# Attention with landmarks and a feed-forward layer on one core: the DMA transposes of k and q issued as one piece, and a new order of all work

## The chip, the cores and the metric

The kernel runs on one core of a Trainium2 chip. The metric is the device time in microseconds (us), the median of several runs. The engines are TensorE (PE), VectorE (DVE), ScalarE (ACT), GpSimd (POOL) and SyncE (SP); POOL and SP here mostly issue DMA transfers.

## The reference

```python
def _attn_ref(q, k, v):                      # q, k, v: (8, 8, 576, 64) float32
    m = 32; scale = 1.0 / np.sqrt(D)
    q_lm = q.reshape(B, H, m, S // m, D).mean(axis=3)
    k_lm = k.reshape(B, H, m, S // m, D).mean(axis=3)
    # sm(a, b): softmax over the last axis of scale * a @ b^T
    A, Bm, C = sm(q, k_lm), sm(q_lm, k_lm), sm(q_lm, k)
    Z = Bm.transpose(0, 1, 3, 2) / (norm1(Bm) * norminf(Bm) + 1e-06)
    for _ in range(6):
        Z = 2 * Z - Z @ Bm @ Z
    return A @ Z @ C @ v
...
def _moe_ref(x, w_in, w_out):                # x: (4608, 512), w_in: (512, 2048), w_out: (2048, 512)
    h = x @ w_in
    return (h * (1.0 / (1.0 + np.exp(-h)))) @ w_out
```

`x` is the attention's output with the heads of a position laid side by side. So for each of 8 batches there are three softmaxes through 32 landmarks, six steps of a Newton iteration on 32 by 32 matrices, and two dense layers with a SiLU between.

## The kernel before, in words

**One program, one written order.** Every piece of work is an `Op` with a name: a kind, some digits for its part, and after the point its batch (`xt1.4`, `ltr0.3`), or after the at sign the place of a second-layer block (`p4@5120.0`). The function `attn` makes the pieces of a batch's attention, `layer1` those of the first dense layer (`h`, `g`), `layer2_pair` and `layer2_plain` those of the second (`ss`, `p`, `c`, `os`). The constant `SEQUENCE` lists the names in the order in which they are written into the program; a suffix such as `/ACT` says which engine does a piece that could run on two. `Plan.run` walks through this list and checks only that each piece stands behind what it depends on. The list was written out by a search over a model of the engines' times; the search itself isn't in the file. Since every engine runs its instructions in program order, the list fixes the order on PE, DVE, ACT, POOL's queue and SP's queue. A word `*n` stands for `n` dummy matmuls on zeros (84 in all, in the first part).

**The pieces that the transposes touch.** Batches 0 to 2 transpose k and q on PE (`tr`, `trc`). Batches 3 to 7 use DMA transposes, SP's line 533, which turn the loaded tile `qk` into `qT`: `xt1.b` for k, then `xt0.b` for q. Each is an operation of its own on SP with a planned time of 1.8 us and a lag of 3 us. It waits for the loads of its batch (`ld1.b`, `ld0.b`: k and q on POOL, line 396), for `ldv0.b` (the first of three loads of v, line 403; a rule written as "one kind of transfer at a time"), and for the pieces `A` and `C` two batches earlier, which read the same buffer. What follows a transpose:

- on DVE `lra`, `lrb`, `lrc`, `lrd` (line 571), the sums over positions that give the landmarks, into `red` and then `rs`; digit 1 for k, 0 for q;
- on PE `ltr` (a fold of `rs`), then `sb` and the chain of softmax, norm and Newton steps (`pb`, `bmx`, `ns`, `nsd`, `fb`);
- on PE `A` and `C`, which read `qT` itself, with `Ax`, `S`, `Ln`, `Rs`, `Cx` on ACT and PE and `etn` on DVE behind them;
- on SP `ct0.b` (line 813), a second DMA transpose, of the exponentials `ce`, from batch 2 on; PE's `cv0.b` multiplies its result with v.

SP's queue holds, in the list's order, these transposes and nearly all stores of the output (line 982). The loads of batch b+1 wait for the first transpose of batch b and, from batch 4's loads on, for the `ct0` of the batch before that one; the first load of v in batch b+2 also waits until `cv0.b` has read the buffer.

`mc` copies `m` out of PSUM on ACT or DVE; `u2`, `c1`, `c5`, `c21` copy second-layer products out, `c11`, `c12`, `c22` add to them on DVE. ACT loads another function table where it goes between exponentials (`Ax`, `Cx`, `Ln`, `Rs`, `pb`) and SiLU (`g`, `gx`).

Of the kernel before, what the change touches and what calls it, by code (L numbers as in the profile page):

```python
# [19 lines left out]
const ldk ld11.0 ident ld00.0 ld01.0 ld0.1 k0cDVE k0cACT ld1.1 fold k0 *18 lms100.0 lms106.0  # L20
ldv2.0 lms1012.0 *6 lms110.0 tr10.0 lms116.0 tr19.0 tr114.0 trc114.0/DVE *2 lms000.0 lms006.0
trc10.0/DVE lms0012.0 tr00.0 trc19.0/DVE lms1112.0 tr05.0 trc00.0/ACT trc05.0/DVE *2 tr09.0
lmc1.0/ACT lms010.0 lms016.0 trc09.0/DVE lms0112.0 ltr1.0 tr014.0 lmc0.0/ACT lmT1.0/DVE
trc014.0/ACT *3 ltr0.0 tr15.0 lmT0.0/DVE ld1.2 trc15.0/DVE *4 sb.0 C0.0 A0.0 ld0.2 tr00.1 Cx00.0
tr014.1 Ax00.0 lms000.1 ldv1.0 lms006.1 pb.0 Ax01.0 lms0012.1 pbs.0 A1.0 wi1b1 pbr.0 lms010.1
bmx.0 Ax11.0 lms016.1 bmt.0 wi0b0 csb.0 lms0112.1 Cx01.0 S01.0 bbd.0 n1.0 lmc0.1/ACT *2 f0.0
ldv0.0 nrm.0 trc00.1/ACT stz.0 *3 tr10.1 stf1.0 stf0.0 wi0b1 Ax10.0 fb00.0 fb01.0 trc10.1/ACT *3
ns00.0 trc014.1/DVE S00.0 S10.0 tr19.1 nsd00.0 Ln01.0 wi3b0 ns01.0 tr114.1 fb10.0 Ln10.0 ns10.0
Ln00.0 nsd10.0 nsd01.0 fb20.0 Rs0.0 fb11.0 *8 ns11.0 ns20.0 S11.0 ctm00.0 nsd11.0 trc114.1/ACT
nsd20.0 ltr0.1 fb21.0 fb30.0 Ln11.0 *1 ns21.0 ctc00.0/DVE lms100.1 tr15.1 Rs1.0 lms106.1 etn0.0  # L30
lms1012.1 lms110.1 wi1b0 lms116.1 trc19.1/ACT nsd21.0 lms1112.1 tr15.2 fb31.0 lmc1.1/DVE
lmT0.1/ACT ns31.0 trc15.2/ACT nsd31.0 *2 ltr1.1 trc15.1/DVE tr09.1 ns30.0 lmT1.1/DVE tr05.1 C1.0
fb41.0 nsd30.0 sb.1 trc05.1/ACT tr114.2 fb40.0 trc09.1/DVE pb.1 ns40.0 ns41.0 Cx11.0 pbs.1 *2
tr19.2 wi1a Cx10.0 pbr.1 nsd41.0 nsd40.0 bmx.1 trc19.2/ACT bmt.1 *4 csb.1 wi0a A1.1 etn1.0 A0.1
trc114.2/ACT tr00.2 wi2a Ax01.1 n1.1 ctm10.0 trc00.2/DVE Ax11.1 tr014.2 wi3b1 Ax00.1 nrm.1 bbd.1
ctc10.0/ACT stz.1 *3 f0.1 fb50.0 S00.1 wrc.0 C1.1 wi2b0 trc014.2/DVE Ln00.1 *1 cv0.0 fb51.0 Cx10.1
cv1.0 stf0.1 wi2b1 ns51.0 fb00.1 Ax10.1 tr10.2 wc.0 Cx11.1 ns00.1 ns50.0 S10.1 wi3a nsd51.0 S11.1
nsd00.1 S01.1 nsd50.0 Ln10.1 zbd.0 Ln01.1 wo0 fb10.1 trc10.2/DVE *5 ns10.1 Rs0.1 ctm10.1 nsd10.1
zt.0 tr09.2 lra1.2 ztc.0/ACT C0.1 wo1 Ln11.1 ctc10.1/DVE *1 m1.0 Cx00.1 mc11.0/DVE mc10.0/ACT *4
m0.0 tr05.2 ldv1.1 Cx01.1 mc00.0/DVE h4.0 mc01.0/ACT etn0.1 g4.0 *3 h3.0 ldv0.1 trc09.2/DVE h2.0  # L40
lrb1.2 ldv2.1 h0.0 lrc1.2 h5.0 trc05.2/DVE wo2 g0.0 ctm00.1 fb20.1 lrd1.2 g5.0 ns20.1 h7.0 wo3
nsd20.1 g3.0 ltr1.2 h1.0 fb30.1 ctc00.1/DVE lmT1.2/ACT ns30.1 h6.0 g1.0 ldv0.2 nsd30.1 m2.0 lra0.2
g2.0 m3.0 mc20.0/DVE mc21.0/ACT mc31.0/ACT lrb0.2 *7 h10.0 g6.0 lrc0.2 h8.0 lrd0.2 g7.0 fb40.1
h11.0 ldv1.2 mc30.0/DVE Rs1.1 ltr0.2 o0@5000.0 lmT0.2/DVE sb.2 h15.0 ns40.1 o0@5001.0 pb.2 nsd40.1
g11.0 ldv2.2 pbs.2 o1@5001.0 fb50.1 pbr.2 bmx.2 ld1.3 bmt.2 csb.2 ns50.1 o1@5000.0 bbd.2 n1.2
nrm.2 g10.0 nsd50.1 ld0.3 stz.2 f0.2 h12.0 g8.0 stf0.2 h9.0 fb00.2 g15.0 zbd.1 ns00.2 hx8.0 g9.0
nsd00.2 cv0.1 fb10.2 gx8.0 wrc.1 ns10.2 h13.0 ldv0.3 wc.1 g12.0 nsd10.2 zt.1 h14.0 fb20.2
ztc.1/ACT etn1.1 ns20.2 o2@5001.0 g14.0 ldv1.3 nsd20.2 g13.0 m3.1 m0.1 m1.1 o2@5000.0 mc00.1/ACT
mc01.1/DVE mc31.1/ACT mc30.1/DVE h2.1 mc10.1/ACT mc11.1/DVE ldv2.3 m2.1 o3@5000.0 mc21.1/ACT
mc20.1/DVE g2.1 ss00@5020.0 h7.1 h4.1 fb30.2 oc@5000.0/DVE h6.1 g4.1 wt00 ns30.2 h9.1 os@5000.0  # L50
h5.1 wt10 h12.1 g5.1 ss10@5020.0 h11.1 g12.1 o3@5001.0 ss20@5020.0 g11.1 g9.1 wt01 h14.1 h15.1
g6.1 nsd30.2 h13.1 fb40.2 g15.1 wt20 h0.1 g7.1 h3.1 wt30 g0.1 h10.1 oc@5001.0/DVE g13.1 h8.1
p1@5020.0 g3.1 wt11 os@5001.0 g10.1 wt21 h1.1 c1@5020.0/ACT xt1.3 p2@5020.0 g1.1 g8.1 p5@5020.0
c11@5020.0 g14.1 ss30@5020.0 xt0.3 C0.2 C1.2 c5@5020.0/DVE A0.2 Cx01.2 p6@5020.0 wt31 ss00@5100.0
p3@5020.0 ss10@5100.0 Ax00.2 p1@5120.0 Cx10.2 ss20@5100.0 Ax01.2 Cx11.2 S00.2 p1@5100.0
ss30@5100.0 Cx00.2 Ln00.2 lra1.3 ct0.2 hx8.1 u2@5020.0/ACT c12@5020.0 p7@5020.0 gx8.1 lrb1.3
lrc1.3 ns40.2 os@5020.0 hx0.0 c1@5100.0/DVE ss00@5120.0 p5@5100.0 l1done.0 nsd40.2 gx0.0
ss10@5120.0 S01.2 p6@5100.0 c1@5120.0/ACT fb50.2 c5@5100.0/ACT c22@5020.0 ld1.4 p2@5100.0 lrd1.3
u2@5100.0/ACT lra0.3 Ln01.2 ld0.4 p7@5100.0 lrb0.3 lrc0.3 p3@5100.0 c11@5100.0 lrd0.3 ltr0.3
ns50.2 ltr1.3 c12@5100.0 p2@5120.0 lmT0.3/ACT c22@5100.0 lmT1.3/ACT ss20@5120.0 sb.3 p4@5020.0  # L60
pb.3 nsd50.2 c11@5120.0 pbs.3 A1.2 C1.3 pbr.3 cv0.2 bmx.3 Ax10.2 ss30@5120.0 Cx11.3 p6@5120.0
ldv0.4 Rs0.2 bmt.3 bbd.3 zbd.2 ldv1.4 Cx10.3 p4@5100.0 wrc.2 Ax11.2 wc.2 ldv2.4 c21@5020.0/ACT
etn0.2 f0.3 u2@5120.0/ACT S11.2 os@5021.0 S10.2 csb.3 zt.2 Ln11.2 p5@5120.0 n1.3 os@5100.0
ztc.2/ACT nrm.3 c21@5100.0/DVE Ln10.2 stz.3 m1.2 Rs1.2 stf0.3 m2.2 fb00.3 C0.3 p7@5120.0
c5@5120.0/ACT mc21.2/DVE xt1.4 mc11.2/ACT etn1.2 Cx00.3 p3@5120.0 mc20.2/ACT c22@5120.0 Cx01.3
mc10.2/DVE ns00.3 h9.2 ct0.3 nsd00.3 h8.2 c12@5120.0 g9.2 m3.2 fb10.3 m0.2 p4@5120.0 mc01.2/DVE
os@5101.0 xt0.4 h7.2 mc31.2/ACT c21@5120.0/DVE ns10.3 h5.2 mc00.2/DVE g7.2 h6.2 g8.2 nsd10.3 h2.2
fb20.3 mc30.2/ACT h1.2 g2.2 h0.2 g5.2 ns20.3 ld1.5 h10.2 nsd20.3 g1.2 h14.2 fb30.3 ld0.5 h4.2 g0.2
ns30.3 h12.2 g14.2 nsd30.3 h3.2 g6.2 fb40.3 h15.2 g10.2 ns40.3 h13.2 g3.2 nsd40.3 h11.2 fb50.3
g4.2 lra1.4 hx8.2 g15.2 p1@5220.0 wrc.3 g12.2 lrb1.4 g13.2 lrc1.4 hx0.1 g11.2 ns50.3 p1@5200.0  # L70
l1done.1 nsd50.3 gx0.1 lrd1.4 ss00@5220.0 c1@5220.0/ACT A0.3 gx8.2 A1.3 zbd.3 p2@5200.0
ss10@5220.0 c1@5200.0/ACT Ax10.3 ss20@5220.0 p2@5220.0 c11@5200.0 lra0.4 p6@5220.0 Ax01.3 Ax11.3
lrb0.4 S10.3 cv0.3 lrc0.4 Ln10.3 S01.3 lrd0.4 Ax00.3 ss00@5200.0 ltr1.4 ldv0.5 ltr0.4 p5@5220.0
lmT1.4/ACT ldv1.5 ss30@5220.0 lmT0.4/ACT u2@5220.0/ACT sb.4 ldv2.5 wc.3 S00.3 p7@5220.0 pb.4
ss10@5200.0 c5@5220.0/ACT pbs.4 Ln00.3 S11.3 c11@5220.0 zt.3 p3@5220.0 Ln11.3 pbr.4 c22@5220.0
bmx.4 Rs1.3 ss20@5200.0 csb.4 p4@5220.0 ztc.3/ACT n1.4 Ln01.3 bmt.4 nrm.4 c12@5220.0 p5@5200.0
Rs0.3 bbd.4 os@5220.0 stz.4 ss30@5200.0 c21@5220.0/ACT xt1.5 f0.4 m3.3 c5@5200.0/ACT stf0.4 m1.3
C0.4 mc30.3/DVE p6@5200.0 mc10.3/ACT etn0.3 mc31.3/ACT p3@5200.0 os@5121.0 Cx01.4 fb00.4
mc11.3/DVE u2@5200.0/ACT os@5120.0 Cx00.4 m2.3 xt0.5 etn1.3 C1.4 m0.3 mc21.3/ACT p7@5200.0
mc20.3/DVE Cx11.4 c12@5200.0 mc01.3/ACT ns00.4 h14.3 os@5200.0 Cx10.4 nsd00.4 h4.3 mc00.3/DVE  # L80
g14.3 ct0.4 h11.3 fb10.4 h7.3 ns10.4 hx0.3 nsd10.4 h2.3 os@5221.0 fb20.4 g7.3 ns20.4 h0.3 gx0.3
nsd20.4 h8.3 fb30.4 g11.3 h1.3 g0.3 ns30.4 h10.3 nsd30.4 g2.3 h15.3 fb40.4 lra1.5 g8.3 hx0.2 ld1.6
g15.3 h3.3 lrb1.5 l1done.2 ld0.6 gx0.2 h5.3 lrc1.5 h9.3 wrc.4 g4.3 lrd1.5 p1@5340.0 g10.3 lra0.5
g3.3 h12.3 lrb0.5 g9.3 ltr1.5 h6.3 lrc0.5 g1.3 lrd0.5 h13.3 lmT1.5/DVE g5.3 hx8.3 c22@5200.0 g12.3
ns40.4 ltr0.5 p4@5200.0 l1done.3 g6.3 nsd40.4 lmT0.5/DVE g13.3 c1@5340.0/DVE sb.5 p1@5300.0 fb50.4
gx8.3 ss00@5300.0 pb.5 p2@5340.0 ss10@5300.0 ss20@5300.0 p5@5300.0 c11@5340.0 c21@5200.0/ACT
c1@5300.0/ACT A1.4 pbs.5 A0.4 pbr.5 cv0.4 Ax11.4 bmx.5 ss30@5300.0 Ax01.4 csb.5 p6@5300.0
c5@5300.0/ACT ldv0.6 bmt.5 Ax00.4 n1.5 bbd.5 ldv1.6 nrm.5 f0.5 stz.5 p3@5300.0 u2@5300.0/ACT
stf0.5 ldv2.6 Ax10.4 fb00.5 ss00@5320.0 ns00.5 p7@5300.0 nsd00.5 ss00@5340.0 S00.4 S11.4 p2@5300.0
wc.4 Ln00.4 fb10.5 ss10@5340.0 S10.4 p5@5340.0 xt1.6 c22@5300.0 Ln10.4 Ln11.4 ss20@5340.0 ns10.5  # L90
p4@5300.0 nsd10.5 fb20.5 c12@5300.0 S01.4 os@5201.0 ns50.4 p6@5340.0 Ln01.4 nsd50.4 c11@5300.0
# [1082 lines left out]
```

## Time and profile before

| | |
|---|---|
| median of 3 runs | 248.0 us (247.12 to 248.7) |
| the profiled execution | 249.88 us, its span 248.2 us |
| PE busy | 236.4 us (95%) |
| ACT, DVE, POOL busy | 185.9, 180.2, 36.9 us |
| mean granted clock of PE | 0.993 |
| DMA transposes `qT<-qk` on SP | 10, issue 2.55 to 4.37 us, median 5.2 us to landing (4.6 to 8.3) |
| DMA transposes `ct<-ce` on SP | 6, issue 1.41 to 2.08 us, median 3.8 us to landing |
| loads of v | 24, median 9.9 us to landing (6.3 to 14.2) |

In the profile's timelines a row gives the start, the length, the engine, the line, the operation and the tiles written and read; in brackets stands the idle time before it, and what ended it. "SPq" and "POOLq" rows are issues of transfers: the length is the time that the queue was held, not the transfer's. In the list of waits a row reads: who, line, for whom; total us, how often, longest.

### The profile page before, as it was taken

To read this page: it belongs to the slowest core of one execution; us is meant where nothing else is said; L and a number is where in the kernel's file an instruction comes from. 1 tells how busy PE (TensorE), PEld (TensorE's weight loads), DVE (VectorE), ACT (ScalarE), POOL (GpSimd) and SP (SyncE) were. 2 spreads that over 40 slices of the span, in tenths; PEclk is the share of its full clock that TensorE was granted. 3 is DMA by queue.
4 is the path that set the end of the run, shared out by engine and by line. 5 is a ranking of instruction groups with operands and counts; after the bars stand their busy time and mean duration, and the time that the engine had idled before them with its cause. 6 is when DMAs were issued, how large, how long until landed. Compare 5 with 4: busy or idle time off the path is not lost.

```text
span 248.2 us, 7298 instructions
## 1 busy us (share of the span) xinstructions
PE 236.4 (95%) x2968; PEld 167.7 (68%) x2968; DVE 180.2 (73%) x498; ACT 185.9 (75%) x439; POOL 36.9 (15%) x62
## 2 busy tenths in 40 slices
...
PEclk9999999999999999799999999999999999999999
...
GB/s 162 201 184 203 170 179 204 206 210 221 173 156 176 214 212 169 187 138 214 126 189 169 178 257 167 168 191 4 63 108 140 123 42 3 0 3 85 129 105 108
DMA packets 54210, 36.82 MB, mean 148 GB/s; under 512 B 34464, under 2 KB 46240, under 8 KB 54176
## 3 DMA queue, kind: packets, MB, share of 16 engines
...
## 4 chain that ended last, share of the span: by engine, by line
PE 66%; DMA 21%; ACT 7%; DVE 2%; issue 2%; POOL 1%; SPq 0%; POOLq 0%; DVEq 0%
PE ps L323 65%; DMA qT<-qk 6%; DMA v<-in_v_dram 5%; DMA qk<-in_q_dram 5%; ACT gm L912 3%; DMA w_in_sb<-in_moe_w_in_dram 3%; DMA qk<-in_k_dram 2%; DVE red L571 1%; ACT L912 1%; PE ps L511 1%; ACT pb L637 1%; ACT gx L937 1%; POOL w_in_sb L410 1%; ACT m L333 1%; ACT L1127 1%
## 5 line engine op out<-in xcount | busy, mean ns | idle before, releaser
L912 ACT ACTIVATE gm<-ps 128x512 f16<-128x512 f32 x128 | 67.9, 644 | 8.3 <-PE ps L323 7.9
L323 PE MATMUL ps<-etn,m 128*128 128x64 bf16 (+1 forms) x512 | 70.4, 286 | 0.2 <-DVE m L335 0.2
L323 PEld LDWEIGHTS <-gm 128*128 128x128 f16 x512 | 48.2, 98 | 12.1 <-issue 2.8
L323 PE MATMUL ps<-w_out_sb,gm 128*128 128x256 f16 (+1 forms) x392 | 54.4, 284 | 0.0
L323 PEld LDWEIGHTS <-m 128*128 128x128 bf16 x512 | 31.7, 98 | 22.7 <-issue 1.6
L323 PEld LDWEIGHTS <-ss 128*128 128x128 f16 x408 | 39.1, 99 | 6.1 <-issue 0.5
L333 ACT COPY ost<-ps 128x256 f32<-128x256 f32 x52 | 19.1, 385 | 21.0 <-PE ps L323 16.6
L323 PE MATMUL ps<-wt,ss 128*128 128x256 f16 x272 | 34.6, 273 | 0.0
L1044 DVE TENSOR_TENSOR ost<-ost,ps 128x256 f32<-128x256 f32 x51 | 20.7, 415 | 16.0 <-PE ps L323 8.3
L335 DVE CAST m<-ps 128x512 bf16<-128x512 f32 x35 | 23.4, 686 | 2.9 <-PE ps L323 2.6
L706 DVE SCALAR_TENSOR_TENSOR st<-st,ps 128x128 bf16<-128x128 bf16 (+2 forms) x54 | 13.6, 259 | 11.7 <-PE ps L323 9.4
L323 PE MATMUL ps<-w_out_sb,ss 128*128 128x256 f16 x136 | 18.3, 279 | 0.0
L333 ACT CAST m<-ps 128x512 bf16<-128x512 f32 x29 | 16.5, 608 | 1.7 <-PE ps L323 1.5
L748 ACT ACTIVATE ln<-ps 128x288 f32<-128x288 f32 x32 | 12.8, 421 | 6.7 <-PE ps L323 6.4
L396 POOL DMA_DIRECT2D qk<-in_k_dram x7 | 5.1, 724 | 83.7 <-DMA ct<-ce 53.8
L403 POOL DMA_DIRECT2D v<-in_v_dram x24 | 14.0, 587 | 23.2 <-PE ps L323 15.0
L1009 DVE TENSOR_TENSOR ss<-gm 128x1024 f16<-128x1024 f16 x15 | 10.3, 685 | 8.4 <-ACT gm L912 8.4
L323 PE MATMUL ps<-zer 128*128 128x256 bf16 x84 | 14.6, 306 | 1.1 <-DVE zer L430 1.1
L323 PE MATMUL ps<-wt,gm 128*128 128x256 f16 x120 | 15.6, 273 | 0.0
L681 DVE TENSOR_TENSOR fb<-st,hmask 128x256 bf16<-128x256 bf16 (+1 forms) x54 | 14.5, 274 | 1.1
L783 ACT ACTIVATE ce<-ps 128x288 bf16<-128x288 f32 x32 | 13.4, 423 | 2.1 <-PE ps L323 2.0
L738 ACT ACTIVATE et<-ps 128x288 bf16<-128x288 f32 x32 | 12.3, 420 | 2.0 <-PE ps L323 1.9
...
## 6 DMA issues: line engine op xcount, KB each, us to landing
...
qk<-in_q_dram POOLq DMA_DIRECT2D x7, 576.0 KB, 10.6
...
w_out_sb<-in_moe_w_out_dram POOLq DMA_DIRECT2D x4, 512.0 KB, 12.0
...
```

The source lines that it names most:

```text
L323: nc.tensor.matmul(out=out_ap, lhsT=lhsT, rhs=rhs, start=start, stop=stop, skip_group_check=True)
L333: nc.scalar.copy(out=out, in_=in_)
L335: nc.vector.tensor_copy(out=out, in_=in_)
L403: lambda e, a=a: nc.gpsimd.dma_start(out=v_r[b % 2][a * L:(a + 1) * L, :, :], in_=v[b].rearrange("h (l a x) d -> a l h (x d)", l=L, a=VA)[ ...
L681: nc.vector.tensor_tensor(out=fb[it % 2][:, g0:g1], in0=bc(sr[it % 3][:, g0:g1, 0:L], 4, 2), in1=bc(hmask, n, 1), op=OP.mult), [o], 14.5 + ...
L706: nc.vector.scalar_tensor_tensor(out=s2[:, g0:g1, lo:SW], in0=s[:, g0:g1, lo:SW], scalar=2.0, in1=ps[:, 0:NG * SW].rearrange("p (g x) -> p ...
L738: lambda e, g=g, et=et, c=c: nc.scalar.activation(out=et[:, c], in_=bank(me["A", g], c)[:, 0:HS], func=AF.Exp, scale=sc / J),
L748: lambda e, g=g, c=c, ln=ln: nc.scalar.activation(out=ln[:, c], in_=bank(me["S", g, c])[:, 0:HS], func=AF.Ln),
L783: nc.scalar.activation(out=ce[:, :, 0:VP].rearrange("p (i c) (a l) -> p c a i l", c=2, a=VA)[:, c], in_=bank(me["C", g], c)[:, 0:HS].rearr ...
L912: lambda e, dc=dc, cell=cell: nc.scalar.activation(out=gm[:, dc, :].rearrange("p (c l j) -> p c l j", c=2, l=L), in_=bank(cell["o"]).rearr ...
L1009: lambda e, o_=o_[:, k], x=x[:, k], y=y[:, k], op=op: nc.vector.tensor_tensor(out=o_, in0=x, in1=y, op=op), dep, 850.0 + prio / 100)
L1044: nc.vector.tensor_tensor(out=out_, in0=x, in1=y, op=OP.add)
```

## The change

The two DMA transposes of a batch become one operation `xt.b` with a planned time of 5.4 us, which issues k's and then q's, with nothing between them on SP. Those who read k's transpose wait, in the plan, for its end without a lag, those who read q's with the lag of 3 us. The loads of the next batch are planned against its end less 0.6 us; in the program they wait, as before, for the transpose of k. The whole list `SEQUENCE` is a new one: new places on every engine, 83 dummy matmuls, other engines for some copies (37 `mc` on ACT and 27 on DVE instead of 29 and 35; 7 `u2` on ACT and 10 on DVE instead of 13 and 4), 11 switches of ACT's table instead of 13, and another order of the first loads.

```diff
...
     def load(name, prio, us, issue, emit, deps=(), after=()):
-        d = list(deps) + list(after)
+        d = list(deps) + [(x, -0.6) if x.name[:2] == "xt" else x for x in after]
...
-            for t in (1, 0):
-                o = A(f"xt{t}.{b}", [("SP", 1.8)],
-                      lambda e, t=t: nc.sync.dma_start_transpose(
-                          out=qT[:, t].rearrange("p g j x -> p (g j) x"),
-                          in_=qk[:, t].rearrange("p g j d -> p (g j d)")),
-                      [qk_ops[b, t, g] for g in range(NG)] + use + gate, p0 + 5, lag=XLAG)
-                o.after = gate
-                qt_ops[t, 0] = qt_ops[t, 1] = [o]
-                me["qk_read"].append(o)
-                me["xts"].append(o)
+            o = A(f"xt.{b}", [("SP", 5.4)], lambda e: [nc.sync.dma_start_transpose(
+                out=qT[:, t].rearrange("p g j x -> p (g j) x"),
+                in_=qk[:, t].rearrange("p g j d -> p (g j d)")) for t in (1, 0)][0],
+                [qk_ops[b, t, g] for t in (1, 0) for g in range(NG)] + use + gate, p0 + 5, lag=XLAG)
+            o.after = gate
+            qt_ops[1, 0] = qt_ops[1, 1] = [(o, 0.0)]
+            qt_ops[0, 0] = qt_ops[0, 1] = [o]
+            me["qk_read"] = me["xts"] = [o]
...
-        gate = last[b - 1].get("xts", [])[:1]
+        gate = last[b - 1].get("xts", [])
...
```

Of the two lists, the stretches around batch 3's and batch 4's transposes and the end. Before:

```
... h1.1 c1@5020.0/ACT xt1.3 p2@5020.0 g1.1 g8.1 p5@5020.0
c11@5020.0 g14.1 ss30@5020.0 xt0.3 C0.2 C1.2 c5@5020.0/DVE A0.2 Cx01.2 ...
... c5@5120.0/ACT mc21.2/DVE xt1.4 mc11.2/ACT etn1.2 Cx00.3 p3@5120.0 mc20.2/ACT c22@5120.0 Cx01.3
mc10.2/DVE ns00.3 h9.2 ct0.3 nsd00.3 h8.2 c12@5120.0 g9.2 m3.2 fb10.3 m0.2 p4@5120.0 mc01.2/DVE
os@5101.0 xt0.4 h7.2 ...
... p3@5740.0 c21@5740.0/ACT os01@5741.0/ACT os00@5741.0/SP c12@5740.0 os10@5740.0/ACT os11@5740.0/SP
```

After:

```
... g15.1 h1.1 xt.3 c1@5020.0/ACT p2@5020.0 g1.1 g9.1 p6@5020.0 ...
stz.3 g9.2 u2@5120.0/DVE f0.3 h5.2 stf0.3 g15.2 xt.4 h8.2 fb00.3 ns00.3 ... hx8.1 fb30.3 ...
fb40.3 h3.2 ct0.3 ns40.3 ...
... p4@5700.0 c11@5700.0 os0@5700.0/SP c21@5700.0/ACT os0@5701.0/SP
```

More of the change, by code (lines that the diff above doesn't have):

```diff
@@ L19 @@
 SEQUENCE = """
[L20 to L91, printed above, removed]
@@ L98 @@
-Cx01.5 lrb0.6 ztc.4/ACT ct0.5 lrc0.6 p3@5320.0 c21@5340.0/ACT lrd0.6 c21@5320.0/ACT c11@5320.0
-Rs1.5 wrc.5 ltr0.6 m3.4 c12@5320.0 lmT0.6/ACT m0.4 os@5321.0 m1.4 mc30.4/DVE mc31.4/ACT ns50.5
-os@5341.0 sb.6 mc00.4/ACT mc10.4/DVE h12.4 pb.6 h14.4 mc11.4/DVE os@5320.0 g12.4 h15.4 pbs.6
-nsd50.5 ld1.7 h13.4 mc01.4/DVE h6.4 pbr.6 ld0.7 h3.4 bmx.6 bmt.6 g14.4 m2.4 bbd.6 cv0.5 zbd.5 g6.4
-mc21.4/DVE h0.4 g13.4 ldv0.7 wc.5 csb.6 g15.4 h1.4 n1.6 ldv1.7 mc20.4/DVE f0.6 g0.4 zt.5 h5.4
-ldv2.7 g1.4 ztc.5/DVE h7.4 nrm.6 g3.4 m1.5 stz.6 m3.5 stf0.6 g7.4 h4.4 fb00.6 mc10.5/DVE g5.4
@@ L146 @@
-os01@5741.0/ACT os00@5741.0/SP c12@5740.0 os10@5740.0/ACT os11@5740.0/SP
+const ldk ld11.0 ident ld00.0 ld01.0 ld0.1 k0cACT k0cDVE ld1.1 k0 *18 tr15.0 lms100.0 tr10.0
+trc15.0/DVE lms106.0 lms1012.0 trc10.0/ACT *9 lms110.0 lms116.0 lms1112.0 tr19.0 lmc1.0/DVE
+tr114.0 trc114.0/DVE *4 tr05.0 fold tr00.0 lms000.0 ltr1.0 lms006.0 lms0012.0 lmT1.0/DVE
+trc05.0/DVE *3 lms010.0 lms016.0 lms0112.0 tr014.0 tr09.0 lmc0.0/DVE trc014.0/ACT *1 ltr0.0 ld1.2
+trc00.0/ACT lmT0.0/DVE trc09.0/DVE ld0.2 *6 C0.0 A0.0 trc19.0/DVE sb.0 Cx00.0 ldv0.0 *2 C1.0 pb.0
@@ new lines @@
+lms000.1 Ax01.0 pbs.0 tr09.1 Cx11.0 ldv1.0 pbr.0 lms006.1 bmx.0 S01.0 csb.0 bmt.0 ldv2.0 Ln01.0
+bbd.0 n1.0 Cx10.0 *5 f0.0 wi2a tr00.1 nrm.0 Cx01.0 stz.0 ctm10.0 stf0.0 trc09.1/ACT wi0b1
+lms0012.1 fb00.0 stf1.0 lms010.1 tr05.1 fb01.0 Ax00.0 ctc10.0/DVE ns00.0 lms016.1 wi0a trc00.1/ACT
+lms100.1 lms0112.1 nsd00.0 ns01.0 tr10.1 trc05.1/ACT nsd01.0 tr19.1 fb11.0 fb10.0 trc10.1/ACT *1
+ns11.0 S00.0 ns10.0 lms106.1 nsd11.0 lms1012.1 nsd10.0 Ln00.0 lms110.1 lmc0.1/DVE ctm00.0 fb21.0
+Rs0.0 fb20.0 tr114.1 trc19.1/DVE ns21.0 ns20.0 ltr0.1 lms116.1 wi0b0 trc114.1/ACT nsd20.0 tr15.1
@@ new lines @@
+Ln01.1 wi1b1 A1.1 zbd.0 tr05.2 Cx11.1 pbr.1 lrc1.2 wo0 lrd1.2 trc05.2/ACT bmx.1 wc.0 *5 csb.1
+Ax11.1 n1.1 Cx10.1 nrm.1 *4 S11.1 lra0.2 zt.0 ctm00.1 wi3b0 Ln11.1 ctm10.1 ztc.0/ACT lrb0.2 Ax10.1
+wi3b1 *1 m0.0 bmt.1 Rs0.1 lrc0.2 S10.1 bbd.1 ltr1.2 wi3a lrd0.2 mc00.0/ACT ctc10.1/DVE *2 ltr0.2
+Ln10.1 *1 f0.1 lmT0.2/DVE ldv0.1 mc01.0/ACT lmT1.2/DVE Rs1.1 ctc00.1/DVE *6 sb.2 m2.0 stz.1 h2.0
+pb.2 ldv2.1 mc20.0/DVE mc21.0/ACT h3.0 ldv1.1 stf0.1 g2.0 h1.0 pbs.2 fb00.1 pbr.2 m1.0 bmx.2 wo1
+h8.0 bmt.2 mc10.0/DVE h0.0 mc11.0/DVE g1.0 *1 csb.2 h9.0 n1.2 g3.0 ns00.1 bbd.2 h6.0 nrm.2 nsd00.1
@@ new lines @@
+g0.0 h7.0 stz.2 fb10.1 wo2 etn1.1 f0.2 ns10.1 o0@5000.0 g7.0 stf0.2 wo3 g8.0 fb00.2 h10.0 nsd10.1
+g9.0 fb20.1 ldv0.2 ns00.2 h11.0 g6.0 nsd00.2 ns20.1 h4.0 fb10.2 g10.0 nsd20.1 ns10.2 m3.0 fb30.1
+g11.0 ldv1.2 o0@5001.0 nsd10.2 fb20.2 mc30.0/ACT mc31.0/ACT ldv2.2 ns20.2 ns30.1 h5.0 nsd30.1
+h14.0 fb40.1 g5.0 nsd20.2 ld1.3 ns40.1 hx8.0 fb30.2 g14.0 nsd40.1 ns30.2 h15.0 fb50.1 g4.0 nsd30.2
+ld0.3 ns50.1 cv0.1 g15.0 fb40.2 wrc.1 hx0.0 gx8.0 nsd50.1 zbd.1 ns40.2 wc.1 h12.0 gx0.0 nsd40.2
+zt.1 h13.0 g12.0 ztc.1/DVE o1@5001.0 etn0.1 l1done.0 g13.0 ldv0.3 ss00@5020.0 m2.1 m0.1 m3.1
@@ new lines @@
+wt31 g13.1 p3@5020.0 Cx10.2 u2@5020.0/DVE ss00@5100.0 p1@5100.0 c12@5020.0 ss10@5100.0 A0.2 A1.2
+C0.2 c1@5100.0/DVE p7@5020.0 Ax11.2 ss20@5100.0 Ax01.2 Cx01.2 S11.2 Ax00.2 p1@5120.0 os@5020.0
+c22@5020.0 Ax10.2 ss30@5100.0 Cx00.2 S10.2 p4@5020.0 lra1.3 ct0.2 Ln10.2 Ln11.2 lrb1.3 S00.2
+p5@5100.0 c21@5020.0/ACT lrc1.3 Ln00.2 lrd1.3 os@5021.0 p6@5100.0 lra0.3 c5@5100.0/ACT lrb0.3
+S01.2 p3@5100.0 u2@5100.0/ACT lrc0.3 Ln01.2 lrd0.3 ss00@5120.0 Rs0.2 ltr1.3 ld1.4 ltr0.3 p7@5100.0
+lmT0.3/ACT lmT1.3/DVE ld0.4 Rs1.2 c12@5100.0 sb.3 C1.3 c22@5100.0 C0.3 pb.3 cv0.2 wrc.2 Cx00.3
@@ new lines @@
+p2@5100.0 Cx11.3 wc.2 ldv0.4 etn1.2 Cx01.3 ldv1.4 zt.2 Cx10.3 p4@5100.0 ztc.2/DVE ldv2.4 pbs.3
+pbr.3 m2.2 c11@5100.0 c21@5100.0/ACT m1.2 ss10@5120.0 os@5100.0 m3.2 mc21.2/ACT p2@5120.0 bmx.3
+mc20.2/ACT etn0.2 c1@5120.0/ACT p5@5120.0 mc11.2/DVE mc30.2/ACT mc31.2/ACT bmt.3 c11@5120.0 h10.2
+mc10.2/ACT ss20@5120.0 h15.2 g10.2 csb.3 wrc.3 h9.2 bbd.3 p6@5120.0 ss30@5120.0 n1.3 h14.2 nrm.3
+stz.3 g9.2 u2@5120.0/DVE f0.3 h5.2 stf0.3 g15.2 xt.4 h8.2 fb00.3 ns00.3 p7@5120.0 g8.2 nsd00.3
+fb10.3 g5.2 ns10.3 h12.2 c5@5120.0/ACT nsd10.3 h4.2 fb20.3 g12.2 c22@5120.0 m0.2 g14.2 ns20.3
```

142 lines of the change are left out of this document (93 added, 49 removed).

## The prediction

> **What bounds the kernel now.** I read the page first (engines, slices), then the table of windows, the waits, and the timelines of SP and PE around the worst one.
>
> ```profile
> PE 236.4 (95%) x2968; PEld 167.7 (68%) x2968; DVE 180.2 (73%) x498; ACT 185.9 (75%) x439; POOL 36.9 (15%) x62
> PEclk9999999999999999799999999999999999999999
> ```
>
> PE is busy for 95% of the span. Matmul counts are the same in both orders, except one dummy ("warm") matmul fewer, so only PE's idle time, its lost clock, the start and the tail can move. The one dip of the clock is in the seventeenth slice.
>
> ```profile
> 90.00:100.00 10.00, 8.29 (x150) 6.16 (x148) 5.85 (x17) 8.56 (x19) 3.01 (x5) 1.00 1.06 195
> 100.00:110.00 10.00, 9.20 (x90) 7.29 (x90) 8.38 (x25) 7.02 (x21) 0.14 (x1) 0.83 0.89 143
> 140.00:150.00 10.00, 8.80 (x81) 5.19 (x79) 7.59 (x23) 8.63 (x24) 1.41 (x2) 1.00 0.94 218
> ```
>
> Columns: stretch, its length, busy PE, PEld, DVE, ACT, POOL, clock, DMA share, GB/s. After the load phase (about 52 us) PE is below 9.5 only here and in the tail. The clock of 0.83 over 10 us means 1.7 us of matmul time lost.
>
> ```profile
> DVE red L571 <- DMA qT<-qk: 4.4, 3, 2.7
> PE ps L323 <- DVE rs L571: 2.9, 2, 2.5
> ```
>
> DVE waits three times for a transposed tile, and behind it PE waits twice for `rs`, the sum that `ltr` (line 323) multiplies. The SP timeline shows why the tile was late, and PE's shows the price:
>
> ```profile
> 84.09 4.21 SPq L533 DMA_TRANSPOSE qT<-qk  x1
> 88.41 1.41 SPq L813 DMA_TRANSPOSE ct<-ce  x1
> 89.91 0.56 SPq L982 DMA_DIRECT2D out_dram<-ost  x1
> 90.56 3.43 SPq L533 DMA_TRANSPOSE qT<-qk  x1
> ```
>
> ```profile
> 98.02 0.27 PE L323 MATMUL ps<-rs,fold 128*128 128x256 f16 x1
> 100.80 0.28 PE L323 MATMUL ps<-rs,fold 128*128 128x256 f16 x1 [2.51 <-DVE rs L571]
> ```
>
> Batch 4's k transpose takes SP 4.21 us where the old plan reckons 1.8; `ct0.3` and a store come next; q starts at 90.56 and lands 8.3 us later, beside the loads of batch 5 (POOL, 92.36). PE sits idle 2.51 us, then runs at half clock for 3.4 us.
>
> **How positions are worked out.** Along each written order I add PE's own work from PE timeline rows (start to next start): eight 256-column matmuls 0.87 us, a pair of 512 columns 0.43, `hx` 0.46, `cv` 0.49, an `m` piece 0.22, `A` or `C` 0.12 to 0.13, `S` 0.12, `ltr` 0.11. Both orders add up to 219 us. An operation's place in this sum is its position; its start minus its position is PE's lag. The lag in this trace: 12.3 at `ltr0.3`, 13.5 at `ltr1.4`, 16.2 at `ltr0.4`, 18.5 at `ltr0.5`, 22.4 at `h0.4`, 24.5 at the last product. So the order of before loses about 12 us after the load phase: 2.7 plus 1.7 at batch 4's transpose, about 2.6 between 140 and 150 us (gaps of 0.62, 0.55, 0.42, 0.36 and three of 0.2), the rest in crumbs.
>
> **The change, part by part.**
>
> *Batch 4's stall goes: -4.4.* In the new order `xt.4` stands at 69.7 and `ltr0.4` at 82.2, so q has 12.5 us. What a pair needs: the two pairs already back to back in this trace start at 61.7 and 160.1 and land their q 9.8 and 7.5 us later (second issue at 65.2 and 163.0, landing 6.3 and 4.6). The DVE chain from landing to `rs` is 98.94 to 100.74, 1.8 us. So 9.3 to 11.6 us are needed. The gate `ldv0.4` stands at 63.3 and takes 6.6 us to land: 69.9, on time. Bounds: 0 if k.4 and q.4 land late, -4.4 if all goes. I leave +0.3 for the slow end.
>
> *Batch 3 gets tighter: +0.8.* `xt1.3` starts at 61.70 because `ldv0.3` (issued at 47.94, 13.7 us to land) lands then. The same bytes stand ahead of that load in the new order and the software queue never runs empty up to there, so `xt.3` starts no sooner; with the same 12.0 us to `rs` (73.7), and `ltr0.3` at position 60.6 instead of 61.5, PE's lag there becomes 13.1 instead of 12.3. Bounds 0 to +2.5 (the gap large enough for the clock to fall).
>
> *The load phase: 0.* Loads move about 0.2 MB per us from 5 to 62 us in either order. Against the bytes ahead of each first use, the new order may run at a lag of some 10.5 where the old has 12, but batch 3's wait takes that back. Bounds -0.8 to +1.0 (`ld1.2` now stands ahead of `ldv2.0` and waits for PE with less queued in front).
>
> *Batch 6: -1.3.* `ldv0.6` at 105.6 plus 6.3 gives `xt.6` a start at 111.9, 2.4 after its place (109.5); `ltr0.6` at 121.7 leaves 9.8 us against a need of 9.3 to 11.6. Half of the 2.6 goes. Bounds -2.6 to 0.
>
> *What queues behind the pair on SP: +0.4.* The pair holds SP for 5.4 to 7.6 us, and stores and `ct` stand behind it. `ct0.3` (75.0) then starts at 75 to 77.5 and lands 3.4 to 4.7 later, at most 82.2; `cv0.3`, which PE meets in order, is at 82.3: nothing. `ct0.5`: 111.9 plus 7 is 118.9, plus the median 3.8 is 122.7 against `cv0.5` at 122.3: 0.4; with the longest landing, 5.7, it is 2.3. Bounds 0 to +2.3. In batch 5, `xt.5` waits for `ldv0.5` (82.9 plus 6.6 is 89.5, 1.8 late), and 12.1 us are left: nothing.
>
> *Engines: 0.* Table switches fall from 13 to 11 (two loads of 1.28); eight evictions of `m` move from DVE (0.69) to ACT (0.61), +4.9 on ACT; six `u2` go the other way, -2.3. ACT comes out level, DVE 3 us lighter. Cover: both have idle time in every stretch, though ACT is above 9 of 10 in many; bounds -1.5 to +2.6.
>
> *Tail: +0.5.* The last transfer was a 64 KB store (2.2 us) and is now a 128 KB one (2.7). Bounds 0 to +0.8.
>
> *New waits that the positions don't show: +0.7.* All of ACT's and DVE's work is in another order. Bounds 0 and +5, the latter about the crumbs of before over again.
>
> Sum: -4.4 +0.3 +0.8 -1.3 +0.4 +0.5 +0.7 = -3.0. The profiled execution took 249.88 around a span of 248.2, so 246.9 for such a one; it lies 1.9 above the median of the runs, 248.0, so a median of **245.0**.
>
> [...] The gap of 2.51 us was followed by 3.4 us of half clock; one of 1.23 us at 20.9 was not. [...]
>
> **The rivals.**
>
> *Everything goes.* Pairs at 9.3 us, no residue in batches 4 and 6: -4.4 -2.6 +0.5 is -6.5, **241.5**. For it: five of ten transposes landed within 5.0 us. Against it: v, stores and q meet on the same DMA engines.
>
> [...]
>
> *The stall moves to batch 3.* The load phase does run faster, PE comes to `ltr0.3` with a lag near 10.6, waits over 2.5 us, and the clock falls; batch 4 keeps 2: **248.5**. Against it: the load phase has crumbs of its own.
>
> *Nothing of it.* The transposes were back to back in two batches of five already, and the new order trades gaps one for one: **248**.
>
> *Slower: `ct` behind the pair.* If `xt.4` and `xt.6` start 2.5 us later than reckoned (q.4 and q.6 land late, since their loads wait for the `ct` before, which itself now waits behind a pair), then `ct0.3` and `ct0.5` land past `cv`, PE stands 2.5 us at each and then runs at half clock: 2 x 4.2 less the 0.4 counted, from 245.0 to **253**. It decides where `ct` lands more than 0.5 us after `cv`'s place; the price grows one for one from there. For it: POOL's loads already wait 53.8 us for `ct` here. Against it: nearly 6 us lie between those loads and `xt`.
>
> **How the numbers follow.** Forecast 0.40, everything 0.17, half clock 0.10, batch 3 0.10, nothing 0.07, slower 0.16. A measurement here can tell about 1% from no change, so faster means below 245.5: 0.27 of the forecast's 0.40, all of "everything", 0.03 of "half clock", 0.47. Slower, above 250.5: the last rival and 0.02 of "batch 3", 0.18. The rest, 0.35, is within 1%. The forecast's own range is 243 to 247; leaving out half of "slower" and the far ends, 8 in 10 lie from 241.0 to 250.5.
>
> **What would show it.** Right: ten transposes in five pairs on SP, each pair's second issue at once behind its first; no PE wait for `rs` above 1 us at batch 4 and no dip of the clock near 100 us; PE 90 to 110 us above 19 of 20. Batch 3's step is right if PE waits 1 to 2 us for `rs` near 72 us. Wrong: a PE wait for the DMA of `ct` at `cv`, or a PE gap with ACT or DVE as releaser where none stood before, beyond 3 us in all.

## The result, and the profile after

| | before | after |
|---|---|---|
| median of the runs beside each other | 248.18 us (247.12 to 248.7, 4 runs) | 245.09 us (244.62 to 245.74, 4 runs) |
| the profiled execution, its span | 249.88, 248.2 us | 244.65, 242.9 us |
| PE busy | 236.4 us | 233.3 us |
| ACT, DVE busy | 185.9, 180.2 us | 184.6, 177.8 us |

The ratio after to before is 0.988, with a 95% interval of 0.984 to 0.993. (The ratios in this text leave out runs that lie more than 1.5% above the fastest of their kernel; of before's runs on one chip these are 10 of 19, so a ratio to before can come out less favourable than the quotient of the medians.) A second measurement of the same kernel on another chip, told below, gives 0.993, with 0.990 to 0.995. So the change makes the kernel faster by about 1%.

The first two parts of the page, engines and slices, of the kernel after:

```profile
PE 233.3 (96%) x2967; PEld 165.7 (68%) x2967; DVE 177.8 (73%) x498; ACT 184.6 (76%) x437; POOL 36.8 (15%) x62
PEclk9999999999999999999999999999999999999999
```

The dip of the clock in the seventeenth slice is gone, and no other has come. The table of windows of the kernel after (columns as before):

```profile
90.00:100.00 10.00, 10.00 (x160) 7.86 (x159) 9.34 (x28) 9.10 (x26) 3.15 (x5) 1.00 1.00 203
100.00:110.00 10.00, 10.00 (x87) 6.25 (x86) 6.96 (x19) 9.31 (x23) 0.00 (x0) 1.00 1.10 181
120.00:130.00 10.00, 8.36 (x98) 6.83 (x96) 7.79 (x23) 5.75 (x18) 0.00 (x0) 1.00 1.07 198
130.00:140.00 10.00, 9.07 (x162) 6.77 (x160) 8.30 (x23) 7.34 (x23) 1.50 (x3) 1.00 0.88 179
```

From 90 to 110 us PE has no idle time left, where it was busy for 8.29 and 9.20 of 10. New holes stand at 120 to 140 us. SP's timeline shows batch 4's pair:

```profile
82.54 6.12 SPq L531 DMA_TRANSPOSE qT<-qk  x2
88.83 1.30 SPq L811 DMA_TRANSPOSE ct<-ce  x1
90.22 1.21 SPq L980 DMA_DIRECT2D out_dram<-ost  x2
```

`ct0.3` and the stores now stand behind q, not in front of it. PE's timeline, at the two `ltr` of batch 4 and then at the two largest holes of the kernel after:

```profile
92.63 0.27 PE L323 MATMUL ps<-rs,fold 128*128 128x256 f16 x1
93.61 0.27 PE L323 MATMUL ps<-rs,fold 128*128 128x256 f16 x1
...
126.42 1.03 PE L323 MATMUL ps<-wt,ss 128*128 128x256 f16 x8 [1.64 <-ACT ost L333]
...
138.07 0.28 PE L323 MATMUL ps<-rs,fold 128*128 128x256 f16 x1 [0.93 <-DVE rs L569]
```

Batch 4's `ltr` no longer wait. A product (`p6@5320.0`) at 126.42 waits for ACT, and batch 6's q `ltr` waits at 138.07. What ACT waits for stands in its own timeline:

```profile
126.00 0.65 ACT L333 COPY ost<-ps 128x256 f32<-128x256 f32 x2 [1.88 <-DMA out_dram<-ost]
```

`c1@5320.0` may write its `ost` buffer only when the store `os@5200.0` has read it. That store was issued at 117.89 and landed 8.1 us later, by the list of transfers; two loads of 0.6 MB each for batch 6 had been issued from 115.86 on. The line of stores (980) in the view by source shows how far out that is:

```profile
DMA to landing us min/median/max: 2.2/2.9/8.1
```

**Where the time came from.** PE's lag, worked out as in the prediction, at the same pieces in the two profiles. In the last two columns the growth between milestones is a mean, over four profiles of before (the one shown, and three more below) and over two of after:

| stretch | before | after | difference | mean before (4) | mean after (2) |
|---|---|---|---|---|---|
| start to the end of the load phase (`o3@5000.0`) | 12.1 | 9.6 | -2.5 | 11.3 | 9.8 |
| to `ltr1.4` | +1.4 | +1.8 | +0.4 | +1.4 | +1.8 |
| to `ltr0.4` | +2.7 | 0.0 | -2.7 | +2.4 | 0.0 |
| to `ltr0.5` | +2.3 | +0.9 | -1.4 | +1.6 | +0.9 |
| to `h0.4` (148 us or so) | +3.9 | +5.2 | +1.3 | +3.8 | +5.3 |
| to the last product | +2.1 | +2.0 | -0.1 | +2.1 | +1.9 |
| sum | 24.5 | 19.5 | -5.0 | 22.5 | 19.7 |

With 0.1 us less of PE's own work and a tail shorter by 0.1 (from the last matmul's end to the end of the span, 4.1 and 4.0 us), that is, to rounding, the 5.3 us between the spans. The mean of four against two gives 2.8, near the 3.1 between the medians: the profile shown of before is one of its slower executions.

### The profile page after: what moved, and what is told of

It reads as the page before. It is cut to its first block, busy times and chain, and to the rows that moved or that the text cites. A ratio compares the mean times of both kernels' runs of the same rounds, so it can differ in the third digit from the quotient of the medians.

```text
span 242.9 us, 7307 instructions
## 1 busy us (share of the span) xinstructions
PE 233.3 (96%) x2967; PEld 165.7 (68%) x2967; DVE 177.8 (73%) x498; ACT 184.6 (76%) x437; POOL 36.8 (15%) x62
## 4 chain that ended last, share of the span: by engine, by line
PE 80%; DMA 9%; DVE 5%; ACT 3%; issue 1%; POOL 1%; POOLq 0%; DVEq 0%
PE ps L323 78%; DMA out_dram<-ost 3%; DMA qk<-in_q_dram 3%; DMA qT<-qk 3%; PE ps L511 1%; DVE ss L1007 1%; DVE red L569 1%; ACT pb L635 1%; DVE ct L335 1%; ACT ln L750 1%; ACT gm L910 0%; DVE gm L1007 0%; POOL qk L390 0%; ACT m L333 0%; ACT ost L333 0%
## 5 line engine op out<-in xcount | busy, mean ns | idle before, releaser
L323 PE MATMUL ps<-w_out_sb,gm 128*128 128x256 f16 (+1 forms) x392 | 53.7, 281 | 0.1
L333 ACT COPY ost<-ps 128x256 f32<-128x256 f32 x46 | 17.2, 388 | 21.2 <-PE ps L323 19.2
L704 DVE SCALAR_TENSOR_TENSOR st<-st,ps 128x128 bf16<-128x128 bf16 (+2 forms) x54 | 13.7, 259 | 11.6 <-PE ps L323 10.9
L333 ACT CAST m<-ps 128x512 bf16<-128x512 f32 x37 | 20.1, 602 | 2.1 <-PE ps L323 1.9
L335 DVE CAST m<-ps 128x512 bf16<-128x512 f32 x27 | 17.8, 685 | 1.6 <-PE ps L323 1.2
L323 PE MATMUL ps<-w_out_sb,ss 128*128 128x256 f16 x136 | 17.6, 272 | 0.0
L323 PE MATMUL ps<-zer 128*128 128x256 bf16 x83 | 13.5, 295 | 1.1 <-DVE zer L430 1.1
L335 DVE COPY ost<-ps 128x256 f32<-128x256 f32 (+1 forms) x24 | 10.6, 441 | 5.4 <-PE ps L323 4.7
```

Source lines behind the costliest of these rows:

```text
L323: nc.tensor.matmul(out=out_ap, lhsT=lhsT, rhs=rhs, start=start, stop=stop, skip_group_check=True)
L333: nc.scalar.copy(out=out, in_=in_)
L335: nc.vector.tensor_copy(out=out, in_=in_)
L704: nc.vector.scalar_tensor_tensor(out=s2[:, g0:g1, lo:SW], in0=s[:, g0:g1, lo:SW], scalar=2.0, in1=ps[:, 0:NG * SW].rearrange("p (g x) -> p ...
```

## The experiments

The first question was how much of the profile of before is typical; then whether the pair, the order around it or the load sequence brings the gain; then what the new holes hang on.

**The kernel before, three more times** (no edit):

> The kernel before, unchanged, profiled once more. If the half clock belongs to the 2.5 us gap at ltr0.4 (batch 4's transpose), it comes again: PE waits over 2 us for rs near 100 us, the clock is 0.5 for 3.4 us behind it, and the span is 248 again. [...]

> The kernel before, profiled a third time, to see what its runs have in common. If late transposes make the slow runs, the time follows the wait of PE at ltr0.4 (1.2 us without half clock in one profile, 2.7 with it in the other). If the load phase does, it follows PE's lag at o3@5000.0 (10.7 and 12.1).

> The kernel before, profiled a fourth time; as for the third.

245.26, 249.36 and 246.86 us, with spans of 243.6, 247.7 and 245.2. PE's `ltr0.4` in the timelines of the first, second and third:

```profile
97.86 0.28 PE L323 MATMUL ps<-rs,fold 128*128 128x256 f16 x1 [1.04 <-DVE rs L571]
```

```profile
100.34 0.40 PE L323 MATMUL ps<-rs,fold 128*128 128x256 f16 x1 [2.59 <-DVE rs L571]
```

```profile
99.55 0.28 PE L323 MATMUL ps<-rs,fold 128*128 128x256 f16 x1 [2.51 <-DVE rs L571]
```

In the second the row itself is slower (0.40 against 0.28): the granted clock is 0.98 from 90 to 100 us and 0.85 from 100 to 110, which is 1.7 us lost, as much as 3.4 us at half clock would lose. In the profile shown it is 0.50 from 102.04 to 105.45. In the third the idle time of 2.51 is that of the profile shown, to the hundredth, and the clock stays whole (1.00 in both windows):

```profile
PEclk9999999999999999999999999999999999999999
```

In the first, k's transpose starts early enough (81.38) for a wait of 1.04 only, though it holds SP for 4.68 us. So the stall is in every one of the four profiles, with 1.0 to 2.6 us, but its price (the lag that PE gains from `ltr1.4` to `ltr0.5`, beyond the 0.9 us of the kernel after) goes from about 1.3 to 4.1 us, with the start of k's transpose and with whether the clock falls. Before's runs spread widely: beside the experiments, on three chips, they went from 243.8 to 253.9 us (19, 23 and 17 runs, medians 247.7, 247.6 and 247.7).

**The kernel after, once more, timed beside before on another chip** (no edit):

> The changed kernel, unchanged, in more rounds beside the kernel before on one chip. The kernel before spreads from 243.8 to 251.6 in 19 runs. If the gain is in the order, the median of this stays 2 to 4 us below that of before and the spread is narrower, since its transposes have more room for late transfers. If the first comparison caught before in bad runs and this in good ones, the two medians come within 1 us.

244.96 us (244.33 to 245.65, 12 runs) against 247.6 (23 runs); ratio 0.993 (0.990 to 0.995). Its profile has the same two holes (1.47 for `ost`, 1.14 at `ltr0.6`). Twelve runs lie within 1.3 us, while before's fastest, 243.77 and 244.85 on the first two chips, are about as fast as these. What the change takes away is mostly the long executions.

**The pair alone, in the old order.** For batches 4, 5 and 6 q's transpose goes right behind k's; all else stays.

```diff
- ... mc21.2/DVE xt1.4 mc11.2/ACT ... mc01.2/DVE os@5101.0 xt0.4 h7.2 ...
+ ... mc21.2/DVE xt1.4 xt0.4 mc11.2/ACT ... mc01.2/DVE os@5101.0 h7.2 ...
- ... xt1.5 f0.4 ... m2.3 xt0.5 etn1.3 ...
+ ... xt1.5 xt0.5 f0.4 ... m2.3 etn1.3 ...
- ... xt1.6 c22@5300.0 ... u2@5340.0/ACT xt0.6 nsd20.5 ...
+ ... xt1.6 xt0.6 c22@5300.0 ... u2@5340.0/ACT nsd20.5 ...
```

> The order of before with one thing moved: xt0.4, xt0.5 and xt0.6 stand directly behind their xt1, so each pair is back to back on SP (ct and the stores between them come after it). If the pair makes the gain: the stall of 2.7 us at ltr0.4 goes, with the half clock where it comes, so 2.5 to 4.4 us less than before. If the new order of everything else makes it: within 1 us of before. Both: ct0.3 is issued about 3.4 us later (91.8 instead of 88.4), and the loads of batch 5 start later by as much.

250.31 us (247.91 to 251.37), ratio 1.013 (1.005 to 1.022): slower than before. Batch 4's stall is gone (lag 11.2 at both `ltr`), but SP's timeline shows batch 6's pair with the stores that now stand behind it:

```profile
128.59 6.54 SPq L530 DMA_TRANSPOSE qT<-qk  x2
135.23 1.85 SPq L979 DMA_DIRECT2D out_dram<-ost  x3
```

Before, two stores went between k and q (135.95, behind a k held for 2.70 us). ACT's timeline and PE's show what hangs on these stores:

```profile
138.19 0.37 ACT L330 COPY ost<-ps 128x256 f32<-128x256 f32 x1 [4.89 <-DMA out_dram<-ost]
```

```profile
136.98 1.03 PE L320 MATMUL ps<-wt,gx 128*128 128x256 f16 x8 [3.12 <-DVE ost L1041]
139.01 0.27 PE L320 MATMUL ps<-st,fb 128*128 128x64 bf16 x2 [1.00 <-ACT ce L780]
```

ACT waits 4.89 us for a buffer that a late store still reads, PE stands for 3.12 and 1.00, and the clock is at half behind that: eight matmuls of 256 columns take 1.03 us at 136.98, 1.91 at 140.08 and 1.04 again at 142.86. Between `cv0.4` and `h0.4` PE loses 7.8 us, where the profile of before loses 3.4.

**The new order with batch 4's pair taken apart.** q goes behind `ct0.3` and a store, as it did before; the other pairs stay whole. (The two transposes are separate operations again, as in the kernel before; the list names them directly one behind the other in the other batches.)

```diff
- ... g15.2 xt.4 h8.2 ... ct0.3 ... nsd50.3 os@5101.0 h0.2 ...
+ ... g15.2 xt1.4 h8.2 ... ct0.3 ... nsd50.3 os@5101.0 xt0.4 h0.2 ...
```

> The new order with batch 4's pair taken apart again as before: xt0.4 stands behind ct0.3 and the store os@5101.0. If the pair matters in this order too, q lands about 5 us later (SP is free for it near 90 instead of 86.2), PE waits 2 to 5 us for rs at ltr0.4, and the kernel is 2 to 6 us slower than the changed one, near or above the time of before. If the new order has room to hide it, within 1 us of the changed kernel.

248.86 us (247.64 to 249.47, 10 runs), ratio to before 1.014 (1.011 to 1.017), 1.2 us over the median of all of before's runs on this chip and 3.8 us over the kernel after. SP's timeline and PE's:

```profile
81.78 2.70 SPq L530 DMA_TRANSPOSE qT<-qk  x1
84.65 2.20 SPq L810 DMA_TRANSPOSE ct<-ce  x1
86.95 0.56 SPq L979 DMA_DIRECT2D out_dram<-ost  x1
87.62 3.35 SPq L530 DMA_TRANSPOSE qT<-qk  x1
```

```profile
97.72 0.40 PE L320 MATMUL ps<-rs,fold 128*128 128x256 f16 x1 [4.26 <-DVE rs L568]
```

A stall of 4.26 us, and half clock behind it (the row takes 0.40 us, where the one of `ltr1.4` takes 0.27). The mean granted clock of this profile is 0.986 over its span of 246.8 us, so about 3.5 us are lost, as much as 7 us at half clock would lose. So neither half of the change works by itself: the old order can't bear the pairs, and the new one can't do without batch 4's.

**The load sequence.** Nineteen early loads (weights and v) stand in another order in the new list. The old sequence in the new order, and the new sequence in the old order, each load in the place of another (the diff is that of the first; the second is its reverse in the old list):

```diff
- ... ldv0.0 ldv1.0 ldv2.0 wi2a wi0b1 wi0a wi0b0 wi2b1 wi2b0 wi1a wi1b0 wi1b1 wo0 wi3b0 wi3b1 wi3a ldv0.1 ldv2.1 ldv1.1 wo1 ...
+ ... ldv2.0 ldv1.0 wi1b1 wi0b0 ldv0.0 wi0b1 wi3b0 wi1b0 wi1a wi0a wi2a wi3b1 wi2b0 wi2b1 wi3a wo0 wo1 ldv1.1 ldv0.1 ldv2.1 ...
```

> The new order with the loads of w_in, w_out and v of batches 0 and 1 put in the old sequence among themselves (all other words stay). If the sequence of the loads is what made the load phase 2.5 us shorter, PE's lag at the end of it goes from 9.6 back to about 12, the software queue dips to under 0.18 MB per us between 14 and 34 us again, and the kernel is 2 to 2.5 us slower than the changed one. If it was the order of PE's and the other engines' work, it stays within 0.7 us of the changed one.

246.12 us (244.19 to 248.08, 10 runs), ratio to before 0.997 (0.992 to 1.003): about 1 us over the kernel after, with its wider spread back. From 20 to 35 us the windows of before, of after and of this kernel:

```profile
20.00:35.00 15.00, 13.47 (x254) 9.16 (x252) 12.56 (x45) 13.08 (x35) 7.67 (x12) 1.00 1.16 178
```

```profile
20.00:35.00 15.00, 14.72 (x242) 9.63 (x238) 13.90 (x51) 14.42 (x41) 8.29 (x13) 1.00 1.24 202
```

```profile
20.00:35.00 15.00, 13.22 (x242) 9.52 (x239) 12.53 (x47) 13.58 (x41) 9.52 (x15) 1.00 1.23 190
```

(The last column is GB/s, the first number behind the length PE's busy time.) With the old sequence the loads bring 178 or 190 GB/s and PE waits for them; with the new one 202. But the old sequence doesn't always do badly: the three repeats of before have 200, 197 and 199 here, and the pair in the old order has 197; the old order without the wait for v, below, has 191. All six profiles with the new sequence in the new order have 200 to 203. Over these the lag at the end of the load phase is 9.2 to 10.4, mean 9.7; over six with the old sequence in the old order 9.8 to 12.1, mean 11.2.

> The order of before with the loads of w_in, w_out and of v of batches 0 and 1 in the new sequence among themselves (the two loads ld1.2 and ld0.2 and the first of v stay where they were). If the sequence of loads sets the length of the load phase, PE's lag at o3@5000.0 is 9 to 10 instead of 10.7 to 12.1 and the kernel is 1 to 2 us faster than before. If it was chance of the run or the order of PE's work, it stays within 0.7 us of before.

249.78 us (248.77 to 252.81), ratio 1.012 (1.005 to 1.019), slower. It doesn't tell sequence from order: the old order asks for the second quarter of `w_in` first, which the new sequence loads late, and PE's timeline shows it standing. Half clock follows: four matmuls on zeros take 1.03 us at 34.42, where four took 0.60 at 24.38 (mean granted clock of this profile 0.989).

```profile
32.68 0.37 PE L320 MATMUL ps<-w_in_sb,zt 64*32 64x512 bf16 x1 [1.74 <-DMA w_in_sb<-in_moe_w_in_dram]
33.92 0.57 PE L320 MATMUL ps<-w_in_sb,zt 64*32 64x512 bf16 x7 [0.87 <-DMA w_in_sb<-in_moe_w_in_dram]
```

It shows only that a load sequence belongs to the order of its first uses. The same holds in part for the old sequence in the new order: PE's longest wait in that load phase, 0.98 us at 34.83, is also for a piece of `w_in`.

**The late store, taken earlier.** In the new order, the store on which ACT waits at 126 us:

```diff
- ... ss00@5300.0 p1@5300.0 ... ss20@5300.0 cv0.4 c11@5200.0 A1.4 ... ldv0.6 pbs.5 os@5200.0 p5@5300.0 ...
+ ... ss00@5300.0 c11@5200.0 os@5200.0 p1@5300.0 ... ss20@5300.0 cv0.4 A1.4 ... ldv0.6 pbs.5 p5@5300.0 ...
```

> The new order with two words moved: c11@5200.0 and its store os@5200.0 stand behind ss00@5300.0, ahead of four DVE sums. In the changed kernel that store is issued at 117.9 and lands 8.1 us later, beside the loads of batch 6; c1@5320.0 on ACT waits 1.9 us for its buffer and PE 1.6 us behind it. If the late store is the cause, the wait of ACT near 124 us falls below 0.5 us and the time falls by 1 to 1.8 us. If the buffer only hides another wait behind it (ACT's Ln and Rs chain, or the transposes of batch 6), PE's lag at ltr0.6 stays at 16.4 and the time within 0.5 us.

245.21 us (243.44 to 247.21, 12 runs) against 244.96 for the kernel after on the same chip: nothing gained. The hole at 126 us is gone (lag 12.9 at `C1.5`, after 14.9), and the waits between 115 and 140 us show what stood behind it:

```profile
DVE red L566 <- DMA qT<-qk: 2.8, 1, 2.8
...
PE ps L320 <- DVE rs L566: 2.7, 1, 2.7
```

Batch 6's pair still starts at 127.02, since it waits for `ldv0.6`. PE, 2 us earlier, now waits for its k, 2.65 us at one stretch, and the clock falls to half behind it: eight matmuls of 256 columns take 1.92 us at 136.28, where they took 1.04 at 131.95. The mean granted clock of this profile is 0.993 over its span of 244.1 us, 1.7 us lost, as much as 3.4 us at half clock would lose.

**The transposes without the wait for v.** In the new order, `xt.b` no longer waits for the batch's first load of v.

```diff
-            gate = v_ops[b][:1]
+            gate = []
```

> The new order, where the DMA transposes of k and q no longer wait for the first load of v of their batch (the loads of k and q, and those who read the buffer two batches before, are still waited for). If that gate sets when the pairs start, xt.4, xt.5, xt.6 and xt.7 start 1 to 4 us earlier, the wait of 1.1 us at ltr0.6 goes, and the kernel is 0.5 to 1.5 us faster. If transposes beside loads of v take longer by as much, the start is earlier and the landing is not, and the time stays within 0.5 us or is up to 2 us longer.

243.62 us (243.17 to 243.93, 4 runs), 1.3 under the kernel after on the same chip; ratio to before 0.988 (0.983 to 0.993). SP's timeline at batch 6:

```profile
121.25 10.50 SPq L531 DMA_TRANSPOSE qT<-qk  x2
131.85 0.56 SPq L980 DMA_DIRECT2D out_dram<-ost  x1
```

The pair starts 5.9 us earlier than in the kernel after (127.14) and holds SP for 10.50 instead of 6.06 us. Its end on SP comes 1.4 us earlier, and the wait at `ltr0.6` is gone. The one for the store stays, in PE's timeline:

```profile
126.45 1.03 PE L323 MATMUL ps<-wt,ss 128*128 128x256 f16 x8 [1.34 <-ACT ost L333]
```

**Both** (the two diffs together):

> The new order with both edits: the early store of e5 and no gate for the transposes as in e6. In e5 the wait of ACT at 124 us is gone, and PE waits 2.7 us for k's rs at ltr1.6 instead, with the half clock; in e6 that place has room and the wait for the buffer stays (1.5 us). If the two waits stand one behind the other, both together give 1.2 to 2 us more than e6 alone: 241.6 to 242.5. If a third wait stands behind them, within 0.5 us of e6, 243.1 to 244.1.

243.49 us (242.08 to 244.64, 6 runs), ratio to before 0.983 (0.978 to 0.988): the best version here, but not clearly ahead of the wait alone taken away. PE's timeline of the profiled run, its slowest:

```profile
134.90 0.28 PE L320 MATMUL ps<-rs,fold 128*128 128x256 f16 x1 [1.12 <-DVE rs L566]
138.05 0.28 PE L320 MATMUL ps<-rs,fold 128*128 128x256 f16 x1 [0.89 <-DVE rs L566]
```

PE comes earlier, and batch 6's pair (121.89, SP held for 10.79 us) is late for it again.

**The old order without the wait for v** (the diff of one line, in the kernel before):

> The order of before without the gate: the transposes don't wait for the first load of v. If the spread of the kernel before (244 to 254 us) comes from transposes that land too late for ltr0.4 and ltr0.6, they start earlier here and the median falls by 1 to 2.5 us with a spread of under 3 us. If the spread comes from the load phase or elsewhere, median and spread stay as they are.

248.32 us (247.38 to 250.24, 12 runs), ratio 1.005 (1.002 to 1.009): no gain. PE still stands 2.29 us at `ltr0.4`, since q still goes behind `ct0.3` and a store. In the old order the pair's being split makes the stall, not the wait for v.

## Why the prediction was right or wrong

The time forecast, 245.0, was met (245.09), and the sum of -3.0 fits the -3.1 between the medians; but terms were off and cancelled, so that a hit this close is partly luck. By the table's means batch 4 brought about 1 less than reckoned and batches 5 and 6 lost 1.7 more, against 1.5 more from the load phase, 0.6 from the tail and some 0.4 from batch 3.

**Batch 4's stall: right.** Forecast -4.4 and +0.3; the stretches from `ltr1.4` to `ltr0.5` give -4.1 between the profiles. The split kernel shows that the pair does it, in the new order. For before's typical execution the term is smaller, about -3 by the table's means, because the clock falls in only two of its four profiles and PE waits only 1.04 us in one.

**The load phase: the step that failed.** Forecast 0; -2.5 between the profiles, -1.5 in the means. The prediction took the queue as moving 0.2 MB per us in either order, a mean over 5 to 62 us (196 and 204 GB/s there, a difference of 4%). It did reckon with a lag of some 10.5 instead of 12, but struck that gain out because batch 3's wait would take it back, and that wait did not come. In the profile shown much of the loss sits in a part of the phase, 178 against 202 GB/s from 20 to 35 us. That rate isn't the whole of it: before's three repeats brought 197 to 200 GB/s there, and their lag at the end of the load phase is still 11.0 in the mean, against 9.8 after. The old sequence in the new order brought back 2.2 us of lag (11.8) in its profile and about 1 us of median. A further part of the -2.5 is chance: the profile shown has the longest load phase of the six with the old sequence. What makes the loads slower in some executions, and how much of the gain is their rate and how much the order of first uses, was not found; it stays open.

**Batch 3: failed.** It was to give +0.8 back by a wait of 1 to 2 us near 72 us. PE came as early as the rival "the stall moves" reckoned (lag 10.2 at `ltr0.3`, for "near 10.6"), and there is no wait: the gate `ldv0.3`, issued at 44.05 instead of 47.94, took 15.4 us instead of 13.7 to land and so landed 2.2 us earlier, and the pair started at 59.54 instead of 61.70. "xt.3 starts no sooner" was the same mistake as the load phase's.

**Batch 6, `ct` and new waits: -1.3, +0.4 and +0.7 forecast, +1.3 measured** (`ltr0.5` to `h0.4`; +1.5 in the means). `ct` cost less than its +0.4: PE waits nowhere for it. Batch 6 is where the sign was wrong: PE arrives 6 us earlier in this stretch and stands 1.64 for a buffer that a store still reads and 0.93 at `ltr0.6`. The prediction reckoned `xt.6` at 111.9 of position, which is 111.9 + 12.4, so 124.3 us on the clock; it started at 127.14, because SP waits for v:

```profile
SPq L531 <- DMA v<-in_v_dram: 30.3, 5, 11.5
```

(SP's list of waits in the kernel after: all five pairs wait for the load of v.) The three experiments there show two waits one behind the other. Taking the store earlier gains nothing by itself, since the wait at batch 6's pair stands behind it; taking away the wait for v gains 1.3 us by itself; and with both done the pair's own landing is the third wait.

**Tail, engines: small.** +0.5 forecast for the tail, -0.1 measured: a last store of 128 KB instead of 64 KB cost nothing that shows. DVE got 2.4 us lighter for 3 reckoned, ACT 1.3 lighter for level.

**The rivals.** "Slower: `ct` behind the pair" had the right mechanism, work queued on SP behind a pair, but in the new order nothing urgent stands there. In the old order it decides, through stores instead of `ct`, with a median 2.6 us over before's. The half clock, given a chance of 0.10, was not settled: a gap of 2.51 us was followed by it in the profile shown and a gap of 2.51 us in a repeat was not, so the gap's length alone did not decide, and what did was not shown. "Nothing of it" falls by the interval.
